# Softmax attention beside linear attention on one core: all score maxima taken directly, more exponential slots, the first rows of x in two halves

## The chip, the cores and the metric

The kernel runs on one core of a Trainium2 chip. A core has TensorE (matmuls, PE in the profile), VectorE (DVE), ScalarE (ACT), GpSimd (POOL) and SyncE (SP), which issues most of the DMAs here. Matmul results go to PSUM, which this kernel uses as eight banks of 128 partitions x 512 float32 numbers. The metric is the device time of one execution in microseconds (us), the median of several runs.

## The reference

Two attention layers over 2048 rows, width 512, 32 heads of 16, written side by side into one output of 1024 columns. A is softmax attention, B is linear attention with a learned feature map:

```python
# A
q, k, v = split_heads(A_x @ A_wqkv)                       # 32 heads, Dh = 16
p = softmax(einsum("bhqd,bhkd->bhqk", q, k) * Dh ** -0.5) # 2048 x 2048 for each head
a = merge_heads(einsum("bhqk,bhkd->bhqd", p, v)) @ A_wo
# B
q, k, v = split_heads(B_x @ B_wqkv)
phi = lambda t: concat([softmax(t @ w_phi), softmax(-(t @ w_phi))])
kv, z = einsum("bhsf,bhsd->bhfd", phi(k), v), phi(k).sum(over s)
b = merge_heads(einsum(phi(q), kv) / (einsum(phi(q), z) + 1e-6)) @ B_wo
return concat([a, b], axis=-1)
```

Almost all the work is in A: for each head a matrix of 2048 x 2048 scores, which has to be made, to have its row maxima taken, to be exponentiated and to be multiplied with v.

## The kernel before

**Units.** A is cut into units: a group of four heads times 256 queries (128 for the first two and the last sixteen units), 73 in all (`units`). Heads are padded to 32 partitions, and each matmul of scores uses half of TensorE's rows, so that two run beside each other.

**Each unit is scored twice.** First with the queries on the partitions (`d_fill`, line 971): 128 queries x 512 keys fill one PSUM bank, VectorE takes the maximum over the 512 keys (line 1084), over two banks in one instruction (a *pair*, 128x1024 in, 128x2 out) or one (a *single*). The maxima of a unit are joined by small POOL operations (`maxima`, line 1116 on), turned by a DMA and written as an extra row into the masked queries QZ. For the last four units VectorE and TensorE do this instead (`maxima_last`). Then the scores are made again with the keys on the partitions and the maximum already subtracted by that extra row (`e_fill`, line 1234), and ScalarE exponentiates one or two banks into slots of a ring `pT` (line 1246; RING = 34 slots of 512 columns). TensorE multiplies the slots with v and a column of ones (`pv_run`, line 1324). For the last three units the sums come from a matmul with ones (line 1319) and VectorE divides (lines 1356 and 1362).

**Combined maxima.** In some units (`zunit`, chosen by ZN/ZD, here 11 units), two heads' maxima are made from four banks at once: TensorE writes scores of key chunk k minus scores of chunk k + 2 (with the negated queries QN, line 978), ScalarE stores the relu of that difference as zS (line 1011), and VectorE adds the scores of chunk k + 2 and takes the maximum in one instruction (line 1078). This is 22 instructions, each in place of four banks of plain maxima, because max(a, b) = max(a - b, 0) + b.

**The order.** Nothing is scheduled at run time. When the program is built, a planner (`_Account`) steps through an account of its own in which each engine's operations have costs; `pick_pe` chooses what TensorE does next (a score pair, an exponential's scores, a value batch, a projection, an idle matmul), `choose` what the others do. Its choices depend on thresholds, the table TH, one row for each 60 us of the account: below what lead of VectorE a single bank is taken (SINGLE), how far maxima and exponentials may run ahead (DCAP, ECAP), how many value steps make a batch (PVN), the least activity of TensorE (UA, RF, REPM), for which matmuls are repeated (`again`) or idle ones issued (`fill_mm`). The result is one fixed list of instructions for each engine with semaphore waits. POOL carries B's feature maps beside all this, with ScalarE and VectorE sharing the copies out of PSUM (`evac`, lines 560 and 563).

**The start.** x arrives in five loads (`load_x`), the weights in pieces (`load_w`). x is turned by matmuls with the identity; for the first 512 rows these fill four banks (line 374), then VectorE and ScalarE copy them out (lines 381 and 383), then k and q of the first group are projected (line 710). The masked queries of the first three units come straight from that q bank (`first_qz`, line 734). The slots of `pT` hold x until it is turned.

Of the kernel before, what the change touches and what calls it, by code (L numbers as in the profile page):

```python
# [9 lines left out]
BF = mybir.dt.bfloat16  # L10
# [203 lines left out]
def bass_concat_heads__softmax_full_mha__linear_kernel_hedgehog__prompt_kernel(  # L214
# [10 lines left out]
    ZN, ZD = 1.6, 8  # L225
    RING = 34
# [9 lines left out]
    with contextlib.ExitStack() as es:  # L236
# [91 lines left out]
        def load_x(name, b0, b1):  # L328
            t_xs[name] = P.dma("sp", dsem("xs%d" % name), lambda e: e.dma_start(
                xs[:, b0:b1, :], A_x[0][128 * b0:128 * b1, :].rearrange("(b p) n -> p b n", p=128)))  # L330
# [5 lines left out]
        load_x(2, 4, 8)  # L336
# [27 lines left out]
        t_wqp = pad_copy(WQp, 0, t_wq0)  # L364
# [5 lines left out]

        pe_idle(6, [t_zmv, t_ones])
        for rb in range(4):
            for ct in range(4):
                t_turn = P.op("pe", lambda e, rb=rb, ct=ct: e.matmul(
                    PS[:, ct, 128 * rb:128 * rb + 128], xs[:, rb, ct * 128:ct * 128 + 128], ident[:, :],
                    start=True, stop=True), [t_xs[rb // 2], t_ident] if ct == 0 else [])
        pe_idle(2)
        t_x0 = []
        for ct in range(4):
            if ct % 2 == 0:  # L380
                t_x0.append(P.op("dve", lambda e, ct=ct: e.tensor_copy(xAT[:, ct, 0:512], PS[:, ct, :]), [t_turn]))
            else:
                t_x0.append(P.op("act", lambda e, ct=ct: e.activation(
                    xAT[:, ct, 0:512], PS[:, ct, :], ACT.Copy), [t_turn]))
# [17 lines left out]
        for r in range(4):  # L402
# [8 lines left out]
            {'SINGLE': 1.013, 'ESINGLE': 1.026, 'ZBIAS': 0.274, 'DBIAS': 0.27, 'ZREST': 0.238},  # L411
            {'SINGLE': 0.647, 'UA': 0.441, 'RF': 0.465, 'REPM': 0.115, 'PV_LOW': 6, 'DCAP': 2.442, 'ZBIAS': 0.207, 'BAL': 68.611},
            {'SINGLE': 1.013, 'UA': 0.408, 'REPM': 0.215, 'LHI': 0.119, 'DCAP': 1.302, 'ECAP': 1.815, 'ZBIAS': 0.315, 'DBIAS': 0.27, 'BAL': -28.613},
            {'SINGLE': 1.157, 'UA': 0.408, 'RF': 0.436, 'REPM': 0.215, 'LHI': 0.03, 'PV_START': 5, 'PV_LOW': 5, 'DCAP': 1.302, 'ECAP': 1.815, 'ZBIAS': 0.315, 'BAL': -28.613},
            {'SINGLE': 0.287, 'UA': 0.425, 'RF': 0.532, 'REPM': 0.196, 'LHARD': 0.35, 'LHI': 0.119, 'DCAP': 1.302, 'ECAP': 1.815, 'ZBIAS': 0.315, 'DBIAS': 0.27, 'BAL': -27.419},
            {'SINGLE': 1.157, 'UA': 0.408, 'RF': 0.436, 'REPM': 0.214, 'LHARD': 0.383, 'LHI': 0.03, 'PV_START': 5, 'PV_LOW': 5, 'PVN': 3, 'DCAP': 1.322, 'ECAP': 1.904, 'ZBIAS': 0.315, 'BAL': -27.335},
            {'COL': 0.708, 'SINGLE': 1.157, 'UA': 0.441, 'REPM': 0.196, 'LHI': 0.065, 'PVN': 3, 'DCAP': 2.495, 'ECAP': 1.461, 'ZBIAS': 0.315, 'DBIAS': 0.27, 'BAL': -27.419},
            {'ESINGLE': 1.165, 'RF': 0.62, 'REPM': 0.196, 'LHI': 0.065, 'ECAP': 1.185, 'ZBIAS': 0.049, 'DBIAS': 0.27, 'BAL': -27.419, 'ZREST': -0.23},
            {'ESINGLE': 1.2, 'RF': 0.62, 'REPM': 0.196, 'LHI': 0.122, 'ECAP': 1.185, 'ZBIAS': 0.049, 'DBIAS': 0.27, 'BAL': -27.419, 'ZREST': -0.23},
# [12 lines left out]
        T = _Thresholds()  # L432
        I32 = mybir.dt.int32
        K = _Account(P)
        K.now = 7.6
# [1645 lines left out]
```

## Time and profile before

| | |
|---|---|
| median of 3 runs | 1199.13 us (1198.91 to 1201.43) |
| profiled execution | 1199.05 us, span 1197.3 us |
| VectorE busy | 1170.3 us (98%) |
| ScalarE busy | 1149.8 us (96%) |
| TensorE busy | 1117.4 us (93%), granted clock 0.999 |
| POOL busy | 821.8 us (69%) |
| maxima over scores on VectorE | 842 pairs, 276 singles, 22 combined |

A busy time counts the instructions of an engine with overlap taken out. A group's row gives line, engine, operation, output and input, count, busy time and the mean duration of one, then the idle time before its instructions. A row of a timeline begins with the start and the length of a run of like instructions on an engine; it is named by the first, so shapes can be mixed in it.

### The profile page before, as it was taken

To read this page: it belongs to the slowest core of one execution; us is meant where nothing else is said; L and a number is where in the kernel's file an instruction comes from. 1 tells how busy PE (TensorE), PEld (TensorE's weight loads), DVE (VectorE), ACT (ScalarE), POOL (GpSimd) and SP (SyncE) were. 2 spreads that over 40 slices of the span, in tenths; PEclk is the share of its full clock that TensorE was granted. 3 is DMA by queue.
4 is the path that set the end of the run, shared out by engine and by line. 5 is a ranking of instruction groups with operands and counts; after the bars stand their busy time and mean duration, and the time that the engine had idled before them with its cause. 6 is when DMAs were issued, how large, how long until landed. Compare 5 with 4: busy or idle time off the path is not lost.

```text
span 1197.3 us, 32106 instructions
## 1 busy us (share of the span) xinstructions
PE 1117.4 (93%) x13025; PEld 468.9 (39%) x13025; DVE 1170.3 (98%) x1290; ACT 1149.8 (96%) x1891; POOL 821.8 (69%) x1636
## 2 busy tenths in 40 slices
PE   8998999998999999999999998999999998899998
PEld 3433333343334333333433333333333333345555
DVE  8999999999999999999999999999999999999995
ACT  5898999999999999999999999999999999999997
POOL 8511211227888888888787887888888888888860
PEclk9999999999999999999999999999999999999999
DMA  5011221210002001001000101121112111111120
GB/s 142 9 25 43 42 48 32 43 38 8 8 14 35 8 6 26 13 10 22 12 7 17 25 7 22 22 49 31 29 34 33 35 34 27 20 29 37 33 30 18
DMA packets 104119, 33.61 MB, mean 28 GB/s; under 512 B 86692, under 2 KB 103972, under 8 KB 103972
## 3 DMA queue, kind: packets, MB, share of 16 engines
q1 hardware_dynamic: 102916, 31.31, 13.4%
q8 instruction: 102, 1.67, 0.6%
q14 instruction: 45, 0.37, 0.1%
q10 hardware_dynamic: 1056, 0.26, 0.1%
HBM read 5.26 MB, written 4.19 MB: 8 GB/s over the span
## 4 chain that ended last, share of the span: by engine, by line
ACT 38%; DVE 33%; PE 23%; SPq 2%; issue 1%; POOL 1%; DMA 1%
ACT pT L1246 32%; DVE part L1084 32%; PE PS L1234 7%; PE PS L971 6%; PE PS L1324 5%; PE PS L1419 2%; ACT eB L1639 1%; ACT xAT L560 1%; PE PS L777 1%; ACT zS L1011 1%; ACT X L560 1%; SPq L1392 1%; ACT WQp L560 1%; POOL uB L1588 1%; PE PS L1563 0%
## 5 line engine op out<-in xcount | busy, mean ns | idle before, releaser
L1084 DVE TENSOR_REDUCE part<-PS 128x2 f32<-128x1024 f32 (+1 forms) x1118 | 1130.0, 1079 | 7.6 <-PE PS L971 5.2
L1246 ACT ACTIVATE pT<-PS 128x512 bf16<-128x512 f32 (+1 forms) x1573 | 1027.7, 797 | 21.3 <-PE PS L1234 17.9
L1234 PE MATMUL PS<-QZ,KT 64*128 64x256 bf16 (+1 forms) x4906 | 560.4, 259 | 40.9 <-ACT pT L1246 22.0
L971 PE MATMUL PS<-KT,QZ 64*128 64x512 bf16 x2139 | 484.5, 383 | 26.3 <-DVE part L1084 9.7
L1234 PEld LDWEIGHTS PS<-QZ,KT 64*128 64x128 bf16 x4906 | 245.5, 94 | 323.1 <-ACT pT L1246 161.4
L971 PEld LDWEIGHTS PS<-KT,QZ 64*128 64x128 bf16 x2139 | 126.2, 93 | 198.2 <-DVE part L1084 72.2
L1324 PE MATMUL PS<-pT,VP 128*17 128x256 bf16 (+1 forms) x4672 | 186.7, 261 | 0.9
L1403 POOL TENSOR_TENSOR QT<-X,Yd 128x256 bf16<-128x256 f32 (+1 forms) x70 | 46.8, 668 | 95.4 <-DMA Yd<-Yd 95.1
L1324 PEld LDWEIGHTS PS<-pT,VP 128*17 128x17 bf16 x4672 | 74.9, 88 | 95.2 <-issue 79.0
L1588 POOL TENSOR_TENSOR uB<-uB 128x256 f32<-128x256 f32 (+2 forms) x160 | 83.4, 522 | 10.1
L1591 POOL TENSOR_SCALAR uB<-uB 128x256 f32<-128x256 f32 (+2 forms) x128 | 82.6, 646 | 11.2
L1116 POOL TENSOR_TENSOR dm<-part 128x16 f32<-128x16 f32 (+1 forms) x66 | 15.7, 238 | 91.1 <-DVE part L1084 90.8
L915 POOL TENSOR_TENSOR QZ<-QT,mask 128x512 bf16<-128x512 bf16 (+1 forms) x70 | 65.9, 941 | 15.7 <-PE PS L1234 12.8
L1645 POOL TENSOR_TENSOR xAT<-eB 128x512 f32<-128x512 bf16 x32 | 36.9, 1152 | 40.8 <-ACT eB L1639 40.6
L1677 POOL TENSOR_TENSOR wA<-eB,rB 128x1024 bf16<-128x1024 bf16 x32 | 61.7, 1928 | 2.0
L560 ACT ACTIVATE xAT<-PS 128x512 f32<-128x512 f32 (+3 forms) x83 | 50.1, 617 | 4.4 <-PE PS L1443 2.9
L1648 POOL TENSOR_TENSOR xAT<-xAT 128x256 f32<-128x256 f32 x64 | 36.0, 563 | 5.0
L1563 PE MATMUL PS<-WKp,xBT 128*128 128x512 bf16 x128 | 36.4, 383 | 1.1 <-ACT pT L1246 0.5
L1639 ACT ACTIVATE eB<-uB 128x1024 bf16<-128x1024 f32 x32 | 36.0, 1124 | 0.0
L1419 PE MATMUL PS<-WOp,QT 128*128 128x512 bf16 x120 | 35.8, 384 | 0.1
L1588 POOL TENSOR_TENSOR uB<-xAT,mB 128x512 f32<-128x512 f32 x32 | 33.8, 1057 | 1.8
L1662 POOL TENSOR_TENSOR WQp<-rB,WQp 128x64 f32<-128x64 f32 x96 | 30.6, 319 | 6.4
(113 smaller groups left out, 752.4 us busy)
## 6 DMA issues: line engine op xcount, KB each, us to landing
out_dram<-xAT SPq DMA_DIRECT2D x31, 128.0 KB, 1.8
Yd<-Yd SPq DMA_DIRECT2D x220, 16.0 KB, 2.1
QT<-eB SPq DMA_DIRECT2D x60, 32.0 KB, 2.0
QZ<-mcols SPq DMA_DIRECT2D x110, 1.0 KB
pT<-in_A_x_dram SPq DMA_DIRECT2D x3, 512.0 KB, 7.5
KT<-eB SPq DMA_DIRECT2D x48, 32.0 KB, 2.0
mcols<-stage SPq DMA_TRANSPOSE x69, 2.2
Yd<-Yd SPq DMA_DIRECT2D x60, 8.0 KB, 1.9
```

Of the source, the lines that this page charges most:

```text
L560: return P.op("act", lambda e: e.activation(dst, src, ACT.Copy), tk)
L915: "pool", lambda e: e.tensor_tensor(QZ[:, u % NQZ, :, 0:w], QT[:, g, q0:q0 + w].unsqueeze(1).broadcast_to([128, 2, w]), mask2[:, 0, :].uns ...
L971: return e.matmul(PS[:, b, :], QZ[p:p + 64, u % NQZ, r % 2, qt * 128:qt * 128 + 128], KT[p:p + 64, g, kc * 512:(kc + 1) * 512], start=star ...
L1084: tk = P.op("dve", lambda e: e.tensor_reduce(o, banks_ap(banks), AX.X, ALU.max), dep)
L1234: tok = P.op("pe", lambda e, r=rs[k], b=banks[k], kt=kt, x=x: e.matmul(PS[:, b, x * w:(x + 1) * w], KT[64 * (r // 2):64 * (r // 2) + 64, g ...
L1246: tk = P.op("act", lambda e: e.activation(pT[:, s0:s0 + n, :] if n > 1 else pT[:, s0, :], banks_ap(banks), ACT.Exp, scale=0.25), dep)
L1324: tok = P.op("pe", lambda e, r=r, kt=kt, x=x, s=es_[r][1]: e.matmul(PS[32 * r:32 * r + 17, bank, 0:w], VP[:, kt, 4 * g + r, :], pT[:, s, x ...
L1419: return e.matmul(PS[:, b, :], QT[:, i, st * 128:(st + 1) * 128], WOp[:, i, :], start=(i == 0), stop=(i == 7))
L1588: return P.op("pool", lambda e: e.tensor_tensor(o, a, b, op), dep)
L1591: return P.op("pool", lambda e: e.tensor_scalar(o, o, 0.0, None, ALU.max), dep)
L1639: cx["e"] = K.task("act", (0.95, 1.07), lambda eng: P.op("act", lambda e: e.activation(eB[:], uB[:], ACT.Exp), toks(d3)), d3, prio=-0.5, n ...
L1677: cx["phi"] = K.task("pool", (1.95, 1.95 + PLAT), lambda eng: P.op("pool", lambda e: e.tensor_tensor(phiB[k].rearrange("p (g f) -> p g f", ...
```

## The change

- ZN goes from 1.6 to 0.01, so no unit is a `zunit`: all maxima are taken on the scores themselves. QN and zS shrink, and the ring has 38 slots in place of 34.
- The first 512 rows of x are handled in two halves of 256: each half is turned into four banks (of its own), copied out, and the q projection of the first half (256 columns) starts as soon as that half is there. The masked queries of the first two units come from it, those of the third from the second half. Two idle matmuls ahead of the copies go.
- The third load of x waits until the first has landed; all that follows on SyncE's queue goes behind it.
- All rows of TH are new, and the planner's account starts at 6.8 instead of 7.6 with other due times for the first loads.

```diff
-    ZN, ZD = 1.6, 8
-    RING = 34
+    ZN, ZD = 0.01, 8
+    RING = 38
...
-        QN = sb("QN", [128, 2, 2, 128], BF)
+        QN = sb("QN", [128, 1, 2, 4], BF)
...
-        zS = sb("zS", [128, 2, 1024], BF)
+        zS = sb("zS", [128, 1, 512], BF)
...
-        def load_x(name, b0, b1):
+        def load_x(name, b0, b1, dep=()):
...
-        load_x(2, 4, 8)
+        load_x(2, 4, 8, [t_xs[0]])
...
-        for rb in range(4):
-            for ct in range(4):
-                t_turn = P.op("pe", lambda e, rb=rb, ct=ct: e.matmul(
-                    PS[:, ct, 128 * rb:128 * rb + 128], xs[:, rb, ct * 128:ct * 128 + 128], ident[:, :],
-                    start=True, stop=True), [t_xs[rb // 2], t_ident] if ct == 0 else [])
-        pe_idle(2)
+        t_x0 = {}
+        for hf in range(2):
+            for rb in range(2 * hf, 2 * hf + 2):
+                for ct in range(4):
+                    t_turn = P.op("pe", lambda e, rb=rb, ct=ct, hf=hf: e.matmul(
+                        PS[:, 4 * hf + ct, 128 * (rb % 2):128 * (rb % 2) + 128],
+                        xs[:, rb, ct * 128:ct * 128 + 128], ident[:, :],
+                        start=True, stop=True), [t_xs[hf], t_ident] if ct == 0 else [])
+            for ct in range(4):
+                dst_x = xAT[:, ct, 256 * hf:256 * hf + 256]
+                src_x = PS[:, 4 * hf + ct, 0:256]
+                if ct % 2 == 0:
+                    t_x0[hf, ct] = P.op("dve", lambda e, o=dst_x, i=src_x: e.tensor_copy(o, i), [t_turn])
+                else:
+                    t_x0[hf, ct] = P.op("act", lambda e, o=dst_x, i=src_x: e.activation(o, i, ACT.Copy), [t_turn])
+            if hf == 0:
+                t_wqp = pad_copy(WQp, 0, t_wq0)
         for ct in range(4):
...
+            t_q0 = P.op("pe", lambda e, ct=ct: e.matmul(
+                PS[:, 0, 0:256], WQp[:, ct, 0, :], xAT[:, ct, 0:256], start=(ct == 0), stop=(ct == 3)),
+                [t_wqp, t_x0[0, 2], t_x0[0, 3]] if ct == 0 else [])
...
-            {'SINGLE': 1.013, 'UA': 0.408, 'REPM': 0.215, 'LHI': 0.119, 'DCAP': 1.302, 'ECAP': 1.815, 'ZBIAS': 0.315, 'DBIAS': 0.27, 'BAL': -28.613},
+            {'COL': 1.011, 'SINGLE': 0.611, 'ESINGLE': 1.019, 'UA': 0.441, 'LHARD': 0.263, 'LHI': 0.021, 'JOBHOLD': 17.432, 'DCAP': 2.726, 'ECAP': 1.605, 'ZBIAS': 0.261, 'DBIAS': 0.339},
...
+                c0 = 256 if (kind, g, c) == ("q", 0, 0) else 0
...
-                        first_qz(b, t)
+                        first_qz(b, t, [2])
...
+        held.add(0)
+        first_qz(0, T_q0, [0, 1])
```

Three places show how the order moves. First TensorE at the start, from its first matmuls to the first scores (zmv: idle matmuls; pT: x before it is turned; KT,QZ: scores for maxima). Before:

```order
L368 MATMUL PS<-zmv,ones_t 128x512 x6
L374 MATMUL PS<-ident,pT 128x128 x16
L368 MATMUL PS<-zmv,ones_t 128x512 x2
L710 MATMUL PS<-xAT,WKp 128x512 x4
L710 MATMUL PS<-xAT,WQp 128x512 x4
L807 MATMUL PS<-ident,pT 128x128 x12
L971 MATMUL PS<-KT,QZ 128x512 x4
```

And now:

```order
L367 MATMUL PS<-zmv,ones_t 128x512 x6
L376 MATMUL PS<-ident,pT 128x128 x16
L390 MATMUL PS<-xAT,WQp 128x256 x4
L723 MATMUL PS<-xAT,WKp 128x512 x4
L723 MATMUL PS<-xAT,WQp 128x256 x4
L723 MATMUL PS<-xAT,WKp 128x512 x2
L986 MATMUL PS<-KT,QZ 128x512 x4
```

The q projection of the first half stands ahead of k, the turning of the next rows behind the first scores, where half of another k projection comes before them.

Next VectorE at the same place, from the copy of the k weights to the first maxima. Before:

```order
L361 COPY WKp<-wA 128x4x8x16
L361 COPY WQp<-wA 128x4x8x16
L381 CAST xAT<-PS 128x512 x2
L734 TENSOR_TENSOR QZ<-PS,mask 128x2x128 x2
L734 TENSOR_TENSOR QZ<-PS,mask 128x512
L1084 TENSOR_REDUCE part<-PS 128x2 x13
```

And now:

```order
L361 COPY WKp<-wA 128x4x8x16
L384 CAST xAT<-PS 128x256 x2
L361 COPY WQp<-wA 128x4x8x16
L384 CAST xAT<-PS 128x256 x2
L747 TENSOR_TENSOR QZ<-PS,mask 128x2x128 x2
L747 TENSOR_TENSOR QZ<-PS,mask 128x512
L1099 TENSOR_REDUCE part<-PS 128x2 x2
```

The copies of the first half of x now stand ahead of the copy of the q weights, those of the second half behind it.

Last VectorE at the end of the program (zS here: the last units' maxima; Yd: the reciprocal of the sums; QT: the divided output). Before:

```order
L1356 RECIPROCAL Yd<-PS 128x128
L1084 TENSOR_REDUCE part<-PS 128x1
L1362 TENSOR_TENSOR QT<-PS,Yd 128x128
L1084 TENSOR_REDUCE part<-PS 128x1 x3
L1164 TENSOR_REDUCE zS<-part 128x2
L1174 TENSOR_TENSOR QZ<-QZ,PS 128x128
```

And now:

```order
L1099 TENSOR_REDUCE part<-PS 128x2 x3
L1179 TENSOR_REDUCE zS<-part 128x2
L1189 TENSOR_TENSOR QZ<-QZ,PS 128x128
L1371 RECIPROCAL Yd<-PS 128x128
L1377 TENSOR_TENSOR QT<-PS,Yd 128x128
```

The first of the three divisions has moved from between the last maxima to behind them. In the middle, the 22 rows of line 1078 are gone, with pairs of line 1099 (1084 before) in their place.

More of the change, by code (lines that the diff above doesn't have):

```diff
@@ L434, in bass_concat_heads__softmax_full_mha__linear_kernel_hedgehog__prompt_kernel @@
         K = _Account(P)
-        K.now = 7.6
+        K.now = 6.8
         T.set(TH0, TH[:1])
@@ L439, in bass_concat_heads__softmax_full_mha__linear_kernel_hedgehog__prompt_kernel @@
         for e in K.free:
-            K.free[e] = 7.6
+            K.free[e] = 6.8
         K.free["pool"] = 14.0
@@ L472, in bass_concat_heads__softmax_full_mha__linear_kernel_hedgehog__prompt_kernel @@
         free_banks = list(range(NBANK))
-        bank_tok = {ct: t_x0[ct] for ct in range(4)}
+        bank_tok = {4 * hf + ct: t_x0[hf, ct] for hf in range(2) for ct in range(4)}
+        free_banks.remove(0)
         pe_mode = [None]
```

79 lines of the change are left out of this document (37 added, 42 removed).

## The prediction

> **What bounds the kernel now.** I read the page's first part first, then the time split into stretches at the first and the last maximum over scores, then the waits of VectorE, then the groups by shape, and last the timelines of the start and the end. Page, and stretches (from:to, length, then each engine's busy time, the granted TensorE clock, DMA share, GB/s):
>
> ```profile
> span 1197.3 us, 32106 instructions
> PE 1117.4 (93%) x13025; PEld 468.9 (39%) x13025; DVE 1170.3 (98%) x1290; ACT 1149.8 (96%) x1891; POOL 821.8 (69%) x1636
> ...
> 0.00:10.69 10.69, 7.47 (x51) 3.51 (x52) 4.97 (x16) 4.10 (x7) 5.44 (x12) 1.00 0.86 260
> 10.69:60.00 49.31, 48.66 (x427) 19.77 (x428) 48.79 (x51) 39.40 (x65) 34.63 (x38) 1.00 0.18 35
> 60.00:120.00 60.00, 52.81 (x649) 21.08 (x641) 57.95 (x62) 53.84 (x81) 10.53 (x26) 1.00 0.14 34
> 120.00:1181.10 1061.10, 997.31 (x11553) 416.88 (x11553) 1054.70 (x1158) 1042.85 (x1732) 770.69 (x1560) 1.00 0.13 25
> 1181.10:1197.30 16.20, 11.18 (x361) 7.64 (x361) 3.92 (x8) 9.66 (x12) 0.46 (x1) 0.95 0.07 20
> ```
>
> Between the first maximum (10.69) and the end of the last (1181.10) VectorE is busy 48.79 + 57.95 + 1054.70 = 1161.4 of 1170.4 us: 99.2%, with 9.0 us idle in all. ScalarE comes second: from 120 on it is busy 98.3% of the time, but before that it has room. So I treat VectorE as the clock of the middle and cut the span into 10.7 of start, 1161.4 of work, 9.0 of idle and 16.2 of tail. The execution itself took 1199.05, 1.75 more than its span and 0.08 under the median of the runs shown; my sum is made in the span and gets these 1.75 back at the end. What VectorE waits for in the middle is mostly one thing:
>
> ```profile
> DVE part L1084 <- PE PS L971: 5.2, 16, 1.4
> ```
>
> that is, 16 waits for score matmuls, the longest 1.4 us. There is nothing large to win there.
>
> **The combined maxima go.** Groups by shape (count | busy, mean ns of one), and pieces of the timeline that give the step from one instruction to the next, which is shorter than its duration because neighbours overlap:
>
> ```profile
> L1084 DVE TENSOR_REDUCE part<-PS 128x2 f32<-128x1024 f32 x842 | 971.1, 1211 | 6.9 <-PE PS L971 4.8 <-PE PS L978 0.2
> L1084 DVE TENSOR_REDUCE part<-PS 128x1 f32<-128x512 f32 x276 | 177.7, 676 | 0.7 <-PE PS L971 0.5
> L1078 DVE CUSTOM_DVE_ANT_0 zS<-PS,zS 128x1024 bf16<-128x1024 f32 x22 | 26.7, 1213 | 1.1 <-PE PS L1234 0.7 <-PE PS L971 0.2
> L1011 ACT ACTIVATE zS<-PS 128x1024 bf16<-128x1024 f32 x22 | 22.8, 1044 | 0.9 <-PE PS L978 0.2 <-PE PS L971 0.2
> ...
> 558.24 19.27 DVE L1084 TENSOR_REDUCE part<-PS 128x2 f32<-128x1024 f32 x17
> ...
> 1170.43 3.67 DVE L1084 TENSOR_REDUCE part<-PS 128x1 f32<-128x512 f32 x6
> ...
> 352.32 1.22 DVE L1078 CUSTOM_DVE_ANT_0 zS<-PS,zS 128x1024 bf16<-128x1024 f32 x1 [0.24 <-PE PS L971]
> 353.47 0.08 DVE L1078 DVE_READ_ACCUMULATOR2_ANT part<- 128x1 f32 x1
> 353.47 3.01 DVE L1084 TENSOR_REDUCE part<-PS 128x1 f32<-128x512 f32 x4
> ```
>
> Each instruction starts about 0.08 us before its forerunner ends. So a pair (two banks) costs (19.27 - 0.08)/17 = 1.129 us of VectorE, a single (3.67 - 0.08)/6 = 0.598, and a combined one 353.47 - 352.32 = 1.15; reading its accumulator is hidden in the next start. (The last row is named by its first member; it mixes shapes and I use only its start.) A combined maximum covers four banks of scores for 1.15 where two pairs cost 2.26, but ScalarE pays a relu of 1024 columns for it.
>
> Counted over the whole order of the changed program, VectorE now issues 976 pairs and 96 singles (2 x 976 + 96 = 2048 banks, all of them), against 842 pairs, 276 singles and 22 combined (1960 + 88 banks). That is +134 pairs x 1.129 = +151.3, -180 singles x 0.598 = -107.6, -22 x 1.15 = -25.3: **+18.4 us on VectorE**. Taken apart: giving up the combined ones alone costs 22 x (2.26 - 1.15) = +24.4; the thresholds that let fewer singles through give back about 6.0. VectorE is busy 99.2% there, so nothing hides this.
>
> ScalarE loses 22 relus of about 0.93 us in step (22.8 busy, 1.04 each with its overlap), some 20 us. Its exponentials go from 475 doubles and 1098 singles to 432 and 1184 for the same 2048 slots, +43 fixed parts of some 0.05 us, +2. Net about -18: it falls to about 1132 us busy. I price this at nothing for the span, because VectorE is the one that is late next. POOL loses 11 masked copies and 11 small memsets, off the path.
>
> **The 38 slots and the thresholds.** Slots free later or earlier only move when ScalarE and TensorE run the value matmuls; with ScalarE 18 us under its old load this is worth nothing from above. From below it can lower VectorE's idle at most from 9.0 to 0. From the other side the 60 to 120 stretch shows 2.05 us of idle in 60; such a stretch throughout would be 40 us. The ordinary rows (6.4 in the 1061 us after) are nearest, since VectorE's work there is unchanged in kind; I keep the old rate and take off the 1.1 us of waits of the combined maxima: 8, with 4 to 14 for the range. TensorE's repeats and idle matmuls go from 425 to 400 instructions by the counts of the two orders, too few to matter in 1117 us of TensorE.
>
> **The start.** Timeline before, of the engines that matter, and the load that the change holds back:
>
> ```profile
> 4.24 0.65 PE L374 MATMUL PS<-ident,pT 128*128 128x128 bf16 x8
> 5.47 0.62 PE L374 MATMUL PS<-ident,pT 128*128 128x128 bf16 x8 [0.59 <-DMA pT<-in_A_x_dram]
> 5.84 0.29 DVE L361 COPY WQp<-wA 128x512 bf16<-128x512 bf16 x1 [0.93 <-DMA wA<-in_A_wqkv_dram]
> 6.13 1.29 DVE L381 CAST xAT<-PS 128x512 bf16<-128x512 f32 x2
> ...
> 7.48 1.04 PE L710 MATMUL PS<-xAT,WKp 128*128 128x512 bf16 x4 [0.95 <-DVE xAT L381]
> 8.35 1.03 PE L710 MATMUL PS<-xAT,WQp 128*128 128x512 bf16 x4
> 8.55 0.69 ACT L559 ACTIVATE KT<-PS,bias_k 128x512 bf16<-128x512 f32 x1 [1.34 <-PE PS L710]
> 9.22 0.83 PE L807 MATMUL PS<-ident,pT 128*128 128x128 bf16 x12
> 9.42 1.35 DVE L734 TENSOR_TENSOR QZ<-PS,mask 128x256 bf16<-128x256 f32 x3 [2.00 <-PE PS L710]
> 9.98 0.61 PE L971 MATMUL PS<-KT,QZ 64*128 64x512 bf16 x4
> 10.69 10.26 DVE L1084 TENSOR_REDUCE part<-PS 128x2 f32<-128x1024 f32 x9
> 13.27 0.69 ACT L559 ACTIVATE KT<-PS,bias_k 128x512 bf16<-128x512 f32 x1
> ...
> pT<-in_A_x_dram SPq DMA_DIRECT2D x3, 512.0 KB, 7.5
> ```
>
> The first half of the rows is turned by 4.89, and its two copies on VectorE (half of 1.29) fit before the q weights arrive at 5.84, so they are free. The second half's copies then follow the q weights at 6.13 and end near 6.8 instead of 7.42; the q matmuls of the first half fill TensorE meanwhile. The k matmuls start near 6.95 (7.48 before), K is out near 8.75, and the masked q of the first two units, which held the first score matmul back until 9.98, is ready by 8. With the six matmuls that stand ahead of it in TensorE's new order, the first score matmul comes near 8.75 and the first maximum 0.7 later: **9.4, a gain of 1.3**.
>
> The new wait stands on SyncE's queue: the third load of x now goes out when the first has landed (by 4.24), and behind it wait the v weights, two more x loads, the rest of k and q, and the wo loads. Before, such a load took 7.5 us under 260 GB/s of traffic and its rows were turned at 9.22; 512 KB alone at that rate are 2 us. Issued 2.5 us later but with less beside it, I expect it near 8 to 9.3. The next K piece, 4.05 us after that turning began, was ready at 13.96; VectorE's first eight banks now last until 9.4 + 4.5 = 13.9, so any lateness beyond shows as idle there. The gain is between -0.5 and 1.8; I take 1.3 and put 0.3 more idle into the middle.
>
> **The end.** The last score matmul, maxima, exponentials and output before:
>
> ```profile
> 1177.43 0.95 DVE L1356 RECIPROCAL Yd<-PS 128x128 f32<-128x128 f32 x1
> 1178.84 0.28 DVE L1362 TENSOR_TENSOR QT<-PS,Yd 128x128 bf16<-128x128 f32 x1
> ...
> 1178.78 0.39 PE L971 MATMUL PS<-KT,QZ 64*128 64x512 bf16 x1
> 1179.03 1.88 DVE L1084 TENSOR_REDUCE part<-PS 128x1 f32<-128x512 f32 x3
> ...
> 1180.91 7.53 ACT L1246 ACTIVATE pT<-PS 128x1024 bf16<-128x1024 f32 x8
> 1181.76 0.29 DVE L1174 TENSOR_TENSOR QZ<-QZ,PS 128x128 bf16<-128x128 bf16 x1 [0.64 <-PE PS L1168]
> 1188.86 1.94 ACT L1246 ACTIVATE pT<-PS 128x1024 bf16<-128x1024 f32 x2 [0.41 <-PE PS L1234]
> ```
>
> ScalarE is still behind when the maxima end: the last half unit needs 8 slots (4 doubles), yet it runs ten doubles until 1190.80; 6.5 us of output follow. After the last score matmul the order has 88 exponent matmuls before and 76 now, at most 22 and 19 slots, so 3 x 0.47 (a double takes 7.53/8 = 0.94) = 1.4 us less backlog. The first reciprocal and its product (1.1 us of VectorE in steps) move from before the last maximum to behind it, where VectorE stands idle: -1.1 in the middle, 0 in the tail while ScalarE's exponentials cover it, 1.1 if they don't. Tail 16.2 - 1.5 = 14.7; with no backlog at all 1182.05 + 0.2 + 3.8 + 6.5 gives 11.5, with the old backlog and no cover 17.3.
>
> **Sum.** 9.4 + (1161.4 + 18.4 - 1.1 = 1178.7) + 8.3 + 14.7 = 1211.1 of span, + 1.75 = **1212.9 us**, slower by 1.15%.
>
> **Rivals.** (a) *The extra work is swallowed*: VectorE's idle in the middle nearly goes, because ScalarE hands banks back sooner, and the tail shrinks to its floor. 9.4 + 1178.7 + 1 + 11.5 + 1.75 = 1202.4, a little less with a better start: at its best no change. For it: ScalarE's 98.3% in the middle. Against: of 9.0 us only 5.2 are waits long enough to be named, and all must fall together.
> (b) *Faster*: the step of a pair falls because no other engine's traffic on the score banks is as dense. To come out below 1196.7 it must save 16.2 over 976 pairs, 0.017 us of 1.129. Against: the 17 pairs at 558 stand far from any combined maximum and already run at this step. 1190 if it fell by 0.023.
> [...]
> (d) *The new order fits worse*: more VectorE idle from late K pieces and maxima in the first 120 us or from the thresholds, 15 to 20 us more: 1230. For it: 2.05 in the 60 to 120 stretch; against: the other stretches.
>
> **Chances.** Forecast 0.78 (its own range 1206 to 1218), (a) 0.06, (b) 0.03, (c) 0.06, (d) 0.07. The range 1204 to 1220 leaves out (b), (c), (d) and half of (a). A measurement of this kernel tells about 0.2% (2.4 us) from no change; (b) is faster, most of (a) is within it, the rest slower.
>
> **What would show it.** Right: 1072 maxima with steps of 1.13 and 0.60; VectorE busy about 1188 and 8 us idle between first and last maximum; ScalarE about 1132, with its new idle waiting for TensorE; first maximum at 9.4. Wrong: a first maximum later than 10.7 or a K piece that VectorE waits for near 14 (the held load); a granted clock below 1 in the middle; a step of pairs that differs from 1.129; or a tail over 17.

## The result, and the profile after

The changed kernel takes 1213.46 us (median of 4 runs, 1211.72 to 1213.72), beside 1199.80 (1198.91 to 1201.43) for the kernel before on the same chip: a ratio of 1.0103, 95% interval 1.0090 to 1.0115. It is slower by some 12 us; the forecast was 1212.9. The page's first part, and the stretches cut at the first and last maximum as before (from:to, length, busy time and count of PE, PEld, DVE, ACT and POOL, granted clock, DMA share, GB/s):

```profile
span 1209.9 us, 31870 instructions
PE 1113.5 (92%) x12958; PEld 461.2 (38%) x12958; DVE 1186.7 (98%) x1201; ACT 1139.7 (94%) x1915; POOL 815.1 (67%) x1614
...
0.00:9.63 9.63, 7.91 (x40) 3.82 (x40) 5.29 (x18) 3.29 (x6) 4.26 (x11) 1.00 0.74 222
9.63:60.00 50.37, 48.76 (x472) 20.00 (x470) 49.05 (x50) 38.48 (x61) 35.12 (x37) 1.00 0.22 47
60.00:120.00 60.00, 53.49 (x641) 21.93 (x626) 59.99 (x64) 53.58 (x84) 10.52 (x26) 1.00 0.14 34
120.00:1191.55 1071.55, 990.98 (x11347) 406.56 (x11345) 1067.76 (x1064) 1035.15 (x1757) 765.21 (x1541) 1.00 0.13 25
1191.55:1209.90 18.35, 12.33 (x483) 8.92 (x477) 4.63 (x9) 9.23 (x11) 0.00 (x0) 0.98 0.04 11
```

Between first and last maximum VectorE is busy 49.05 + 59.99 + 1067.76 = 1176.8 us and idle 5.1. So the 12.6 us of longer span (1197.3 before) are: start -1.1 (9.63 instead of 10.69), work +15.4, idle -3.9, tail +2.1. (The prediction's cut at 1181.10 stands 0.2 behind the end of the last maximum, 1180.91; cut there, as here, the tail before is 16.4 and its growth 1.9.) All of the loss is VectorE's own work and a longer tail. The profiled execution is the fastest of the four, 1.7 us under the median; where the others spend more stands in no trace. The maxima by shape (count | busy, mean ns of one | idle before), VectorE's and ScalarE's waits for score matmuls, and the chain that ended last by engine:

```profile
L1099 DVE TENSOR_REDUCE part<-PS 128x2 f32<-128x1024 f32 x976 | 1116.0, 1222 | 4.2 <-PE PS L986 3.3
L1099 DVE TENSOR_REDUCE part<-PS 128x1 f32<-128x512 f32 x96 | 62.9, 684 | 0.5 <-PE PS L986 0.2
...
DVE part L1099 <- PE PS L986: 3.4, 8, 1.2
ACT pT L1261 <- PE PS L1249: 29.0, 72, 1.8
...
DVE 43%; ACT 31%; PE 22%; DMA 1%; issue 1%; SPq 0%; POOL 0%
```

The step from one pair to the next has a median of 1.131 us over the whole trace, that of a single 0.598. In the chain VectorE now has 43%; what ScalarE saved shows as waits for its score matmuls, 29.0 us. The same two rows of before:

```profile
ACT pT L1246 <- PE PS L1234: 17.9, 47, 2.1
...
ACT 38%; DVE 33%; PE 23%; SPq 2%; issue 1%; POOL 1%; DMA 1%
```

The start, with TensorE's turning of x drawn out to 2.15 us (0.65 and 0.62 before; the lengths of the single matmuls are in the last section):

```profile
4.21 2.15 PE L376 MATMUL PS<-ident,pT 128*128 128x128 bf16 x16
5.30 0.76 DVE L384 CAST xAT<-PS 128x256 bf16<-128x256 f32 x2 [0.47 <-PE PS L376]
7.20 1.19 PE L723 MATMUL PS<-xAT,WKp 128*128 128x512 bf16 x4
9.20 0.60 PE L986 MATMUL PS<-KT,QZ 64*128 64x512 bf16 x4
9.63 4.68 DVE L1099 TENSOR_REDUCE part<-PS 128x2 f32<-128x1024 f32 x5
15.54 3.55 DVE L1099 TENSOR_REDUCE part<-PS 128x2 f32<-128x1024 f32 x4 [1.23 <-PE PS L986]
```

The end, VectorE (the three reciprocals of the last units) and ScalarE (the last exponentials):

```profile
1187.89 3.66 DVE L1099 TENSOR_REDUCE part<-PS 128x2 f32<-128x1024 f32 x3
1194.80 0.96 DVE L1371 RECIPROCAL Yd<-PS 128x128 f32<-128x128 f32 x1 [2.29 <-PE PS L1339]
1199.26 0.96 DVE L1371 RECIPROCAL Yd<-PS 128x128 f32<-128x128 f32 x1 [3.18 <-PE PS L1339]
1203.88 0.96 DVE L1371 RECIPROCAL Yd<-PS 128x128 f32<-128x128 f32 x1 [3.33 <-PE PS L1339]
1197.58 2.85 ACT L1261 ACTIVATE pT<-PS 128x1024 bf16<-128x1024 f32 x3 [0.99 <-PE PS L1249]
1201.00 1.02 ACT L1261 ACTIVATE pT<-PS 128x1024 bf16<-128x1024 f32 x1 [0.56 <-PE PS L1249]
```

ScalarE's last exponentials wait for their scores here, 0.99 and 0.56 us, and all three reciprocals for the matmuls that sum (line 1339). TensorE has 483 matmuls to do after the last maximum, 361 before.

### The profile page after: what moved, and what is told of

It reads as the page before. It is cut to its first block, busy times and chain, and to the rows that moved or that the text cites. A ratio compares the mean times of both kernels' runs of the same rounds, so it can differ in the third digit from the quotient of the medians.

```text
span 1209.9 us, 31870 instructions
## 1 busy us (share of the span) xinstructions
PE 1113.5 (92%) x12958; PEld 461.2 (38%) x12958; DVE 1186.7 (98%) x1201; ACT 1139.7 (94%) x1915; POOL 815.1 (67%) x1614
## 3 DMA queue, kind: packets, MB, share of 16 engines
HBM read 5.26 MB, written 4.19 MB: 8 GB/s over the span
## 4 chain that ended last, share of the span: by engine, by line
DVE 43%; ACT 31%; PE 22%; DMA 1%; issue 1%; SPq 0%; POOL 0%
DVE part L1099 43%; ACT pT L1261 27%; PE PS L1249 6%; PE PS L986 6%; PE PS L1339 5%; ACT xAT L570 1%; PE PS L707 1%; ACT eB L1654 1%; PE PS L1434 1%; PE PS L723 1%; ACT WQp L570 1%; PE PS L790 1%; ACT X L570 1%; PE PS L1828 1%; PE PS L1578 0%
## 5 line engine op out<-in xcount | busy, mean ns | idle before, releaser
L1099 DVE TENSOR_REDUCE part<-PS 128x2 f32<-128x1024 f32 (+1 forms) x1072 | 1171.5, 1174 | 4.7 <-PE PS L986 3.4
L1249 PE MATMUL PS<-QZ,KT 64*128 64x256 bf16 (+1 forms) x4840 | 566.3, 260 | 38.9 <-ACT pT L1261 17.3
L986 PE MATMUL PS<-KT,QZ 64*128 64x512 bf16 x2096 | 444.8, 384 | 39.9 <-DVE part L1099 24.0
L1249 PEld LDWEIGHTS PS<-QZ,KT 64*128 64x128 bf16 x4840 | 250.1, 94 | 320.3 <-ACT pT L1261 171.8
L986 PEld LDWEIGHTS PS<-KT,QZ 64*128 64x128 bf16 x2096 | 114.4, 93 | 214.9 <-DVE part L1099 117.5
L570 ACT ACTIVATE xAT<-PS 128x512 f32<-128x512 f32 (+2 forms) x84 | 50.5, 622 | 8.0 <-PE PS L1458 4.3
L1603 POOL TENSOR_TENSOR uB<-mB,xAT 128x512 f32<-128x512 f32 x32 | 33.8, 1057 | 1.7
```

The costliest lines, as they stand in the source:

```text
L570: return P.op("act", lambda e: e.activation(dst, src, ACT.Copy), tk)
L986: return e.matmul(PS[:, b, :], QZ[p:p + 64, u % NQZ, r % 2, qt * 128:qt * 128 + 128], KT[p:p + 64, g, kc * 512:(kc + 1) * 512], start=star ...
L1099: tk = P.op("dve", lambda e: e.tensor_reduce(o, banks_ap(banks), AX.X, ALU.max), dep)
L1249: tok = P.op("pe", lambda e, r=rs[k], b=banks[k], kt=kt, x=x: e.matmul(PS[:, b, x * w:(x + 1) * w], KT[64 * (r // 2):64 * (r // 2) + 64, g ...
L1603: return P.op("pool", lambda e: e.tensor_tensor(o, a, b, op), dep)
```

## The experiments

In each, the ratio is to the kernel before on the same chip (1199.8 to 1201.6 us), so 1.0103 is the changed kernel's. A difference of ratios times 1200 is given as us.

### Is VectorE the clock? Work added, work removed

To the kernel before, 22 spare maxima; their cost isn't told to the planner, so the order stays:

```diff
+        spare = sb("spare", [128, 2], F32)
...
+                    tk = P.op("dve", lambda e: e.tensor_reduce(spare[:, 0:2], banks_ap(banks), AX.X, ALU.max))
```

> The kernel before with 22 more pairs on VectorE: behind each of the 22 combined maxima a plain maximum over the same two banks goes to a spare tile, with the order of everything else unchanged. By the step of a pair that is 22 x 1.129 = 24.8 us of VectorE. Theory (VectorE is the clock of the middle, its work adds one for one): 1199.8 + 24.8 = about 1224, not under 1218. Rival (extra work on VectorE is swallowed by its idle time and by a shorter tail): 1200 to 1207.

Measured: 1221.34 us, ratio 1.0184 (1.0158 to 1.0211): 20.4 us more than the kernel before beside it by the medians, 22 (19 to 25) by the ratio, for some 25 us of added steps. The idle in the middle went from 8.9 to 7.6, the tail stayed at 16.4. The chain has VectorE at 55% (33% before). So VectorE's added work costs most of its own length, and only a few us of it, if any, are swallowed.

Then the opposite, on the changed kernel, again with the order unchanged:

```diff
+        pairs = [0]
...
-                    tk = P.op("dve", lambda e: e.tensor_reduce(o, banks_ap(banks), AX.X, ALU.max), dep)
+                    pairs[0] += n == 2
+                    cut = n == 2 and pairs[0] % 24 == 12
+                    src = banks_ap(banks, slice(0, 256)) if cut else banks_ap(banks)
+                    tk = P.op("dve", lambda e: e.tensor_reduce(o, src, AX.X, ALU.max), dep)
```

> The changed kernel with its order unchanged, but 40 of its 976 pairs read 256 columns of each bank in place of 512 (their maxima are over half the keys, so this part of the work is left out). That takes 40 x 512/1024 x 1.067 = about 21 us from VectorE and nothing from any other engine. Theory: 1213.5 - 21 = 1192, or a little more where ScalarE, 1139.7 us busy, becomes the one that is late: 1192 to 1199. Rival (the new order, not VectorE's work, makes the time): stays over 1207.

By the steps in the changed kernel's trace, 1.131 us for a pair and 0.598 for a single, 512 columns are 0.533 us, so the 40 cuts are some 21.

Measured: 1216.89, ratio 1.0137 (1.0112 to 1.0161). Nothing came back; the median is even 4 us up, though the four executions spread from 1214.12, at a mean granted clock of 0.997, to 1220.48, at 0.988. VectorE was busy 1173.2 instead of 1186.7, but idle 20.5 instead of 5.1 in the middle. VectorE's and ScalarE's waits and the chain of this run:

```profile
DVE part L1104 <- PE PS L986: 14.9, 43, 1.4
ACT pT L1266 <- PE PS L1254: 31.9, 73, 1.8
...
ACT 50%; PE 34%; DVE 12%; issue 1%; SPq 1%; DMA 1%; POOL 0%; POOLq 0%
```

"VectorE is the clock" falls in the form that its work comes off the time in both directions. The chain now runs through ScalarE and TensorE.

### What takes over: ScalarE, TensorE's work, or the order?

Three runs. First 40 of the 432 double exponentials at half width, and VectorE untouched:

```diff
+            doubles[0] += n == 2
+            cut = n == 2 and doubles[0] >= 40 and doubles[0] % 10 == 0
...
+                if cut:
+                    tk = P.op("act", lambda e: e.activation(
+                        pT[:, s0:s0 + n, 0:256], banks_ap(banks, slice(0, 256)), ACT.Exp, scale=0.25), dep)
```

> The changed kernel, order unchanged, with 40 of its 432 double exponentials over 256 columns of each bank in place of 512 (the other half of their slots keeps older numbers, so a part of the exponentials is left out): 40 x 0.43 = 17 us less on ScalarE, nothing less on any other. Theory as first put (VectorE alone is the clock of the middle): 1213, unchanged. Rival (ScalarE's chain has become the one that binds, as the run with 40 shortened pairs suggests): 1198 to 1203. Third (the two are interlocked by the fixed order and equally long): 1211 to 1215.

Then these and the cuts in the maxima together:

> Both cuts at once in the changed kernel: 40 pairs (21 us of VectorE) and 40 double exponentials (17 us of ScalarE) over half the columns, order unchanged. If VectorE and ScalarE are interlocked and equally long: 1195 to 1202, a gain that neither cut gives alone. If a third thing binds (TensorE, or the latency from a freed bank to the next scores): 1209 to 1215.

And both with the planner's repeated matmuls left out (`range(R)` becomes `range(1)`, `range(R * m)` becomes `range(m)`), about 14 us of TensorE's work by an estimate from the steps in the changed kernel's trace, 0.22 us for 512 columns and 0.11 for 256, with two score matmuls beside each other:

> The kernel of the run with both cuts, in which the planner's repeated score matmuls are left out of the program too (48 of the maxima's, 164 + 4 of the exponentials'; the rest of the order is the same, and the idle matmuls stay). That is 48 x 0.217/2 + 164 x 0.113/2 = about 14 us less work on TensorE. If TensorE is the third chain beside VectorE and ScalarE: 1192 to 1200. If what is left is the latency of the fixed interlock (a bank freed, the next scores made, their reader started): 1205 to 1210. If the lower activity brings the clock down: over 1212, with a granted clock under 0.99.

ScalarE's steps in that trace are 0.904 us for a double and 0.477 for a single, so 512 columns are 0.427 and the 40 cuts some 17.

Measured: ScalarE alone 1210.51, ratio 1.0087 (1.0065 to 1.0109); both 1208.31, 1.0061 (1.0043 to 1.0079); both and fewer repeats 1206.71, 1.0052 (1.0029 to 1.0076). Cutting either engine by 17 to 21 us gives 2 us or nothing, both together 5. So neither engine alone is the bound of the changed order. The pair of cuts didn't give the 1195 to 1202 that was expected of two engines tied to each other; 1208.31 lies next to the 1209 to 1215 of a third limit. Fewer repeats took another 1 us off the median, inside the interval, but that doesn't clear TensorE's work: the eight executions spread from 1202.65 to 1213.78 as their mean granted clock goes from 0.998 to 0.987; the profiled one has 0.990, where that of the changed kernel has 0.998. The repeats are there to keep TensorE active, and the four executions with both cuts alone had 0.995 to 0.999, so the clock differs along with the work. The two executions without the repeats at 0.998 took 1202.65 and 1203.13, some 4 us less than any with both cuts alone (1207.12 to 1209.46 at 0.995 to 0.999). What TensorE's work alone is worth stays open. With both cut, VectorE still waits 12.3 us for scores and ScalarE 35.6:

```profile
DVE part L1104 <- PE PS L986: 12.3, 35, 1.5
ACT pT L1274 <- PE PS L1258: 35.6, 84, 1.8
...
ACT 36%; PE 33%; DVE 27%; SPq 1%; issue 1%; DMA 1%; POOL 0%; POOLq 0%
```

The theory that was tried next is an interlock. TensorE makes the scores of both engines in one fixed order, through eight banks. An engine that is early finds its next scores queued behind a matmul that waits for a bank of the other, so a lead would be lost within a few steps. The sparse cuts stood at different places for the two engines, so that by this theory mostly only one was early at a time. Its test is cuts of the same size spread over every step: first VectorE's 976 pairs alone, then both engines.

```diff
-                    tk = P.op("dve", lambda e: e.tensor_reduce(o, banks_ap(banks), AX.X, ALU.max), dep)
+                    src = banks_ap(banks, slice(0, 500)) if n == 2 else banks_ap(banks)
+                    tk = P.op("dve", lambda e: e.tensor_reduce(o, src, AX.X, ALU.max), dep)
...
+            made[0] += 1
+            c = slice(0, 500 if made[0] > 60 else 512)
...
-                    pT[:, s0:s0 + n, :] if n > 1 else pT[:, s0, :], banks_ap(banks), ACT.Exp, scale=0.25), dep)
+                    pT[:, s0:s0 + n, c] if n > 1 else pT[:, s0, c], banks_ap(banks, c), ACT.Exp, scale=0.25), dep)
```

> The changed kernel, but every maximum over two banks reads 500 of the 512 columns of each bank (12 keys of each 512 are left out of these maxima); order, waits and all else are as they were. VectorE: 976 maxima x 24 columns, 25 ns each if a column costs what it does between the steps of 1131 and 598 ns, so 24 us less, spread evenly. Theory VectorE is the clock: about 1190 us. Theory interlock (VectorE and ScalarE take turns in TensorE's fixed order, and a lead of either is lost at the next place where the other is last): 1203 to 1211, and VectorE idles about 20 us more in the middle.

> The same as the run with even cuts in VectorE's maxima, and from the 61st exponential on each of those reads and writes 500 of the 512 columns of each bank too (the other columns of the probabilities stay as they were): ScalarE about 400 doubles x 20 ns + 1156 singles x 10 ns, 20 us less, evenly. Theory interlock: with both engines quicker at every step the whole is quicker by most of it, 15 to 20 us: 1193 to 1198 us. Theory of a third limit in TensorE's order (its matmuls and the banks' round trip): stays at 1205 or above. Theory VectorE is the clock: about 1190, as with VectorE's cuts alone.

Measured: VectorE's cuts alone 1210.03, ratio 1.0073 (1.0056 to 1.0090); both 1200.60, ratio 0.9997 (0.9987 to 1.0006). The steps of pairs did fall from 1.131 to 1.106 us, so 24.4 us of VectorE's steps gave 3.6 (some 1 to 6 by the two intervals), its idle in the middle going from 5.1 to 18.5. The two traces are of executions of nearly one length (1211.72 and 1211.86 us), so they show where the cut time went, not the gain. (Its busy time fell by only 14.4: a maximum is 1.191 us long here, against the step of 1.106, and one that isn't overlapped by the next counts with its full length.) With ScalarE's 20 us beside it the same cut gave 12.7 in all. What TensorE waits for shows the hand-over. After, VectorE cut, and both cut (matmul and its line, whose bank it waits for: us in total, times, longest; PEld is the weight load ahead of it):

```profile
PEld PS L1249 <- ACT pT L1261: 171.8, 512, 0.8
PEld PS L986 <- DVE part L1099: 117.5, 325, 0.8
PE PS L986 <- DVE part L1099: 24.0, 78, 0.6
PE PS L1249 <- ACT pT L1261: 17.3, 54, 0.5
```
```profile
PEld PS L1250 <- ACT pT L1262: 213.5, 609, 0.9
PEld PS L986 <- DVE part L1100: 57.8, 169, 0.8
PE PS L1250 <- ACT pT L1262: 27.3, 85, 0.6
PE PS L986 <- DVE part L1100: 9.2, 33, 0.5
```
```profile
PEld PS L1254 <- ACT pT L1266: 187.2, 531, 0.8
PEld PS L986 <- DVE part L1100: 71.5, 208, 0.8
PE PS L1254 <- ACT pT L1266: 22.6, 73, 0.6
PE PS L986 <- DVE part L1100: 11.2, 38, 0.5
```

In these rows TensorE's waits for VectorE's banks fall from 141.5 to 67.0 us (117.5 + 24.0, 57.8 + 9.2), and those for ScalarE's rise from 189.1 to 240.8. With ScalarE quicker too they are 82.7 and 209.8. There are also waits across: before a score matmul of the maxima for a bank that ScalarE still reads (39.2 + 8.7 us in the changed kernel), and before one of the exponentials for a bank of VectorE's (26.2 + 4.6). These are the places where one engine's lateness reaches the other. The single cut came out inside the interlock's 1203 to 1211 and far from the 1190 of a single clock. The double cut came out 3 us above the interlock's 1193 to 1198 and 4 below the 1205 of a third limit: about 13 of 20 us came back, where either engine's cut by itself, even or sparse, gave 4 at most. ScalarE's even cut by itself wasn't run, so that the 13 need both engines rests on its sparse cut (2 us), and the interlock is the likely cause, not a proven one. What holds the remaining 7 wasn't separated. VectorE still idles 15.5 us in the middle there, TensorE still waits longer for ScalarE than in the changed kernel, and the granted clock has a small part: the ten executions go from 1198.92 to 1203.71 while their mean clock goes from 0.997 to 0.992.

### Which part of the change costs what

The kernel before with direct maxima alone (`ZN, ZD = 0.01, 8`; old slots, start and thresholds):

> The kernel before with the combined maxima alone given up (ZN 0.01); ring, thresholds and start are the old ones. The planner's order then has 892 pairs and 264 singles: VectorE's work is 892 x 1.129 + 264 x 0.598 = 1164.9 against 1141.0 before, +23.9. Theory: about 1222 (1217 to 1227), worse than the changed kernel, since the old thresholds keep the singles. Rival (the thresholds or the ring cost the 13 us): 1199 to 1204.

The changed kernel with the old table of thresholds:

> The changed kernel with the old table of thresholds; direct maxima, 38 slots and the new start stay. VectorE's maxima are then 878 pairs and 292 singles, 1165.9 us against 1159.3 in the changed kernel and 1164.9 in the kernel before with direct maxima alone (1230.3). If the new thresholds bring what the changed kernel gains over that run: 1222 to 1230. If the 38 slots and the start bring it: 1213 to 1219.

The changed kernel with the combined maxima and the 34 slots put back, under the new thresholds:

> The changed kernel with the combined maxima put back (ZN 1.6, its tiles, 34 slots), new thresholds and new start kept. VectorE's maxima fall by 20 us (870 pairs, 220 singles, 22 combined), but the planner now sends 38 more copies out of PSUM to VectorE, some 0.55 each, +21. Theory (VectorE's whole work counts, whatever it is made of): 1208 to 1217, no gain, though the combined maxima are back. Rival (giving up the combined maxima is what costs, by some other way than VectorE's work): about 1199.

Measured: direct maxima alone 1230.33, ratio 1.0244 (1.0229 to 1.0260), 3 us above the range that was expected: VectorE is busy 25.9 us longer than before (1196.2), and its idle in the middle (10.4) and the tail (18.0) grow by 1.5 each. All of the change but the thresholds 1227.01, 1.0217 (1.0198 to 1.0235). The third 1345.58, 1.1209. The maxima of the first two and VectorE's waits for them:

```profile
L1084 DVE TENSOR_REDUCE part<-PS 128x2 f32<-128x1024 f32 x892 | 1028.8, 1212 | 9.0 <-PE PS L971 6.1 <-PE PS L1234 0.2
L1084 DVE TENSOR_REDUCE part<-PS 128x1 f32<-128x512 f32 x264 | 171.4, 677 | 1.3 <-PE PS L971 0.7
```
```profile
L1099 DVE TENSOR_REDUCE part<-PS 128x2 f32<-128x1024 f32 x878 | 1012.8, 1211 | 11.5 <-PE PS L986 8.8
L1099 DVE TENSOR_REDUCE part<-PS 128x1 f32<-128x512 f32 x292 | 188.7, 678 | 0.9 <-PE PS L986 0.4
```

Added in this order, the whole splits into +29 us for the direct maxima, -3 for the 38 slots and the new start (the two intervals overlap), and -14 for the thresholds (1.0217 to 1.0103). The thresholds do two things. They turn 196 singles into 98 pairs (292 to 96, 878 to 976), 196 x 0.598 - 98 x 1.131 = 6.4 us of VectorE's steps, and they bring its idle in the middle from 12.3 to 5.1.

The run with the combined maxima put back is far outside both of its expectations and doesn't answer its question: its last maximum ends at 1214 and 129 us follow in which POOL works off B's feature maps that this order had left over.

```profile
1214.00:1343.20 129.20, 35.03 (x513) 16.00 (x513) 17.03 (x34) 20.51 (x26) 99.23 (x178) 0.58 0.13 28
```

The 0.55 us for a copy in the expectation was an estimate; the trace of before shows 0.608 as the step of two copies of 512 columns (from 6.13). The run shows only that this table of thresholds doesn't fit that order; what combined maxima would cost under thresholds of their own stays open.

### The tail and the held load

For the value matmuls of a unit the planner keeps one bank free (`hold`), but the last three units need two each, one for the sums of line 1339. In the changed order the matmuls of all three units stand behind the last score matmul; before, those of two. If the one kept bank is the cause, keeping two brings them forward:

```diff
-                hold = 1
+                hold = 2 if pv_ready[0][0] >= NU - LASTU else 1
```

> The changed kernel with one number of the planner changed, which acts on the last three units alone: it keeps two banks free for their value matmuls in place of one, so that 128 of these stand behind the last score matmul (as before the change) and not 192. Theory (the tail grew from 16.4 to 18.3 us because TensorE has three units' value matmuls to do there): tail 16 to 16.8, time 1211 to 1212. Rival (the tail is ScalarE's backlog of exponentials): tail stays at 18 or more, time 1213.5.

The other run lets the third load of x go at once:

```diff
-        load_x(2, 4, 8, [t_xs[0]])
+        load_x(2, 4, 8)
```

> The changed kernel with the wait taken off the third load of x; the orders of the engines are the same. If the held load makes the second K piece late: the 1.23 us for which VectorE waits at 15.5 go, but the first x rows and the q weights come a little later: first maximum 9.6 to 10.2, time 1212 to 1213.5. If the wait at 15.5 comes from the order of TensorE's work: it stays, and the time is 1213.5 to 1214.5.

Measured: with two banks kept 1211.12, ratio 1.0083 (1.0067 to 1.0098), and a tail of 15.3 us instead of 18.3, with 337 matmuls in it instead of 483:

```profile
1192.96:1208.30 15.34, 9.81 (x337) 6.90 (x329) 3.38 (x7) 8.44 (x10) 0.00 (x0) 0.93 0.04 13
```

The long tail is thus TensorE's leftover value matmuls: the seven other kept traces whose last units have the changed order (with cuts, or with the load not held) have tails of 17.9 to 19.8 us; this one alone is shorter, and shorter than the 16 to 16.8 that was expected. The time fell by 2.4 (the intervals overlap), less than the tail: the stretch from first to last maximum, where these matmuls now stand, took 1184.0 instead of 1181.9, and the first maximum came 0.6 earlier, which the edit doesn't touch (see the last section).

With the load not held: 1212.80, ratio 1.0105 (1.0087 to 1.0123), no difference. The wait of 1.23 us at 15 us, which I would have put down to a late load, stays:

```profile
15.17 2.42 DVE L1099 TENSOR_REDUCE part<-PS 128x2 f32<-128x1024 f32 x3 [1.23 <-PE PS L986]
```

It comes from TensorE's order, not from the load. But the held load has little to spare: in the trace with two banks kept, where the start was 0.6 us quicker, a weight load of TensorE waits 0.74 us, until 11.43, for rows of x from the held queue, and of the 0.6 us only 0.2 are left at the maximum behind the same wait (15.35).

## Why the prediction was right, and where its steps were not

The time came out 0.6 us from the forecast. That closeness is partly luck: the tail came out 3.6 us too long, the work and the idle time 5.1 too short, and the profiled execution, from which the terms are measured, is itself 1.7 under the median. The direction, and the work that makes most of the loss, were not luck. In the span:

| term | predicted | measured |
|---|---|---|
| start, to the first maximum | 9.4 | 9.6 |
| VectorE's work, first to last maximum | 1178.7 | 1176.8 |
| its idle there | 8.3 | 5.1 |
| tail | 14.7 | 18.3 |
| span | 1211.1 | 1209.9 |

- **The combined maxima go: +18.4 on VectorE.** Right in its mechanism. The counts were those of the order, the steps 1.131 and 0.598 where 1.129 and 0.598 were taken. The work grew by 15.4, where 18.4 less the 1.1 of the moved division were expected. That added work is hardly hidden is shown by the spare maxima (20 to 22 us of time for 25 of steps), and that the combined maxima are the part that costs by the run with that edit alone (+29).
- **"I treat VectorE as the clock of the middle."** Enough for work that is added, wrong as a bound: 24 us less of the same engine's steps give back 3.6. The changed order ties VectorE and ScalarE together so closely that either takes over within a few us, and the chain's shares, 33% and 38% before and 43% and 31% after, say so better than the 99% of busy time. At 98% busy VectorE gave nearly nothing back until ScalarE, 94% busy, was cut beside it.
- **ScalarE's 18 us less, priced at nothing.** Its busy time fell by 10 us only (1149.8 to 1139.7; the forecast was 1132), and its waits for scores grew from 17.9 to 29.0. Its work changed as forecast (22 relus gone, and the steps of 0.904 and 0.477 us for a double and a single give +2 for the new counts). Part of the difference is likely counting: behind a wait an instruction doesn't overlap the one before it, and its full length counts as busy (a double has a mean length of 1.069 us beside its step of 0.904), as with VectorE's even cuts. Nothing is about right: 17 us less of ScalarE in the changed kernel give 2 (1.0103 to 1.0087, the intervals overlap).
- **The slots and thresholds: nothing from above, 8 of idle.** The idle was mis-sized by 3.2 us (5.1 measured), inside its 4 to 14. The old rate of idle wasn't what the direct maxima would have had: under the old thresholds it is 12.3. So the thresholds were worth about 14 us, of which the forecast saw only the fewer singles (6.0; 6.4 by the counts of the two orders).
- **The start: 9.4, a gain of 1.3.** It gained 1.1 between two executions in which TensorE's matmuls reached their later, shorter lengths at different times (4.3 us before, 7.6 after), and 1.3 between executions that are alike in this (last section). The held load was no cause of lateness there, as taken, though the prediction put 0.3 on it that it didn't cost. One reading was wrong without effect: 4.05 us after the turning of x the copy of that K piece starts (13.27); it was ready 4.74 after (13.96).
- **The end: 14.7.** This is the term that was wrong, 18.3, outside its own 11.5 to 17.3. The step that failed is the one from 88 and 76 exponent matmuls to 1.4 us less backlog: it counted exponent matmuls behind the last score matmul and no value matmuls. Those, with the matmuls of their sums, grew from two units' to three units' (256 to 384), and TensorE became late where ScalarE had been. The last exponential ended 10.5 us after the last maximum (9.9 before) and 7.8 us followed it, not the 6.5 that the prediction kept. The two-bank run takes 3.0 us of the tail away.
- **The rivals.** (a) fell: idle didn't go to 1 nor the tail to 11.5. (b) fell: the pairs' step is 1.131. (d) fell: idle went down. (c), a lower granted clock in the middle, came up, but small. The stretches of the profiled execution round to 1.00 up to the last maximum, yet in the middle of it the clock is at 0.50 once, for 3.4 us (rows in the last section), behind 3.5 us in which TensorE was busy for 2.18. In the run with 129 us of POOL's leftovers TensorE is busy 35.03 of 129.20 us and the granted clock is 0.58. With the repeated matmuls left out the mean clock was 0.987 to 0.998 beside 0.995 to 0.999. These go together with less work of TensorE; that this is the cause isn't settled by them. In the changed kernel VectorE stays busy through the dip and idles 0.2 us behind it, so the dip explains little of the 12 us.
- **The signs of being wrong.** Three of those that the prediction named came up: the tail is over 17, VectorE waits 1.23 us for a K piece that is ready at 15.1, and the clock falls in the middle (0.50 for 3.4 us). The first was the failed step above. The second has another cause than the one named, and the third was too short to matter.

## What to carry to other kernels

A step's measured length times the count in the new order gave the cost of added work on a saturated engine to within a few us, but the same sum doesn't give what removing work would bring: in this fixed order, which feeds two engines through shared banks, a cut in one engine gave 4 us at most, and only cuts in both, at every step, gave a good part back. In a tail, count every kind of work that stands behind the last matmul of the main stage, not only that of the engine which was last before. Thresholds that steer a planner were worth 14 us here and cost far more in an order that they weren't made for: judge an edit with the old ones and with its own. And a mean granted clock of 1.00 over a long stretch can hide dips, here 3.4 us at 0.50 in 1071.55: look at short windows, and at several executions, before the clock is called constant.

## What the runs showed of the hardware

At the start TensorE's first matmuls, the same instructions in each run, ran at different lengths in single executions. Before, and in the profiled run of the changed kernel (duration in ns, least, median and most; then the idle matmuls ahead of them in the changed kernel):

```profile
L374 PE MATMUL PS<-ident,pT x16: 219/219/256, 4.2 to 5.9; 128*128 128x128 bf16 x16
```
```profile
L376 PE MATMUL PS<-ident,pT x16: 289/314/314, 4.2 to 6.0; 128*128 128x128 bf16 x16
...
L367 PE MATMUL PS<-zmv,ones_t x6: 606/634/634, 1.7 to 3.8; 128*128 128x512 bf16 x6
```

The granted clock of 1.00 in the rows of the start is no measurement. In the kept traces the record of the clock begins only some us into the span, 4.33 before and 7.55 in the changed kernel, and the views count time without a record as 1.00. Of these 128-column matmuls all sixteen of the changed kernel end ahead of the first record and took 289 to 314 ns; the fourteen of before that start behind it took 219 to 230. Shortly after it, projections of 128x512 take 379 in the median, where the idle matmuls of that shape took 606 to 634. In the middle, where the record is complete, one dip of the changed kernel, at 0.50 from 386.43 to 389.85, gives lengths like the early ones (stretches, and matmuls within the dip; over the whole trace the score matmuls of 512 columns have a mean of 384):

```profile
383.00:386.50 3.50, 2.18 (x24) 0.90 (x22) 3.50 (x4) 3.49 (x7) 2.91 (x8) 0.99 0.05 6
386.50:390.00 3.50, 3.50 (x21) 1.27 (x18) 3.50 (x4) 3.15 (x5) 1.50 (x2) 0.52 0.09 14
...
L986 PE MATMUL PS<-KT,QZ 64*128 64x512 bf16 x4 | 1.3, 621 | 0.0
```

So in these two traces TensorE's first matmuls run at about half the later rate: those of 128x512 start 0.43 us apart ahead of the record and 0.22 behind it, those of 128x128 0.11 and 0.055 (in the dip those of 64x256 0.21 to 0.22, over the whole trace 0.109). No clock is recorded for that time. The record begins at different moments in executions whose order is the same up to there, and the first maximum follows it: with the new start it comes at 8.99 and 9.02 where the record begins at 4.53 and 4.64, at 9.25 or 9.26 in the four traces with 5.41 to 5.91 (the one with the load not held is among them), and at 9.30 to 9.63 with 6.64 to 7.55. The old start has 10.69 at 4.33, and 10.54 and 10.52 at 5.01 and 5.26 (the spare maxima, and direct maxima alone). Compared at like moments, near 5.3, the new start gains 1.3; a start read from one traced execution is known to about 0.6 us only.

A lower mean clock goes with a longer execution. Of the nine executions of the kernel before that stand beside the sparse cuts in ScalarE, the four with a mean granted clock of 1.000 took 1198.77 to 1199.86 us, the five with 0.999 to 0.996 took 1200.96 to 1203.10, about 1 us for each 0.001. Which is cause and which effect wasn't tested: matmuls are longer in a dip (621 ns, not 384), but an engine that comes late also leaves TensorE idle (24.0 us ahead of the maxima's score matmuls, for VectorE's banks, in the changed kernel).
